# A new order of steps, new engine flags and new buffer numbers for a two-layer attention kernel on one Trainium2 core

## The chip, the cores and the metric

The kernel runs on one core of a Trainium2 chip. The metric is device time in microseconds (us), measured over whole executions. The engines are TensorE (PE, matrix products), VectorE (DVE), ScalarE (ACT), GpSimd (POOL) and SyncE (SP), which issues transfers (DMA). PEld in a profile is TensorE's weight load, which overlaps PE.

## What is computed

Two attention mixers alternate over x, which has 2048 rows of 512 bf16 values: A, B, A, B, each with layer normalisation ahead and a residual addition behind. Both layers A share their weights, and so do both layers B. There are 32 heads of 16 channels.

```python
def A(x):   # linear attention
    pq, pk = q @ w_phi, k @ w_phi
    phi_q = concat(softmax(pq), softmax(-pq))   # 32 features
    phi_k = concat(softmax(pk), softmax(-pk))
    kv = phi_k^T v                              # over all rows
    z = sum of phi_k over all rows
    return (phi_q kv / (phi_q z + 1e-6)) @ wo

def B(x):   # each row sees 8 rows: itself and 2, 4, ... 14 rows back
    attn = softmax(q . k[idx] / 4, masked where idx < 0)
    return (sum over the 8 of attn * v[idx]) @ wo

x = x + A(ln(x)); x = x + B(ln(x)); x = x + A(ln(x)); x = x + B(ln(x))
```

## The kernel before

x stays in on-chip memory as four blocks b of 512 rows, each with four tiles t of 128 rows. All of the kernel is built from small steps. A step belongs to one engine and issues a few instructions. Function names start with `s_`, and a step's name says its stage, layer L and block b.

- Head: `s_loads` queues the loads of x and the raw weights on SP (L315 to L327), `s_consts` sets constants and issues 14 matmuls that only warm PE (L287), `s_ln_first` normalises the first x, `s_fold` folds `w_phi` into the query part (fold0) and the key part (fold1) of the weight: transposes (L364), a product with `PHI` (L374) and a cast into `WA`.
- Layer A: `s_a1` makes keys (L593) and values (L605), exponentials (L599), their sums and reciprocals, the scaled keys (L651) and the sum kv over all rows (L668). `s_a2` makes the queries (L698), their exponentials `Eq` (L706) and sums (L714). `s_akv` turns kv over once all blocks are in: a cast, transposes (L744), and the products that form `ZM` (L753) and `R` (L757). `s_a3` makes the scale factors `rho` (L782 to L801). Blocks 0 and 1 spread `rho` over partitions by matmuls (L808) and multiply it into `Eq`: DVE either reads PSUM itself (L816), or ACT first copies it to `bs` (L846). Blocks 2 and 3 write `rho` to memory (L824), read it back as `Prho` (L831) and multiply by that (L835). `s_a4` takes the output product (L900) and `s_out`.
- `s_out`: a projection (L520) and the residual addition, either on DVE (L533) or by one more matmul with the identity (L523) and ACT (L530). Squares (L540) and sums give the next normalisation, applied by DVE (L444) or ACT (L446). xn is transposed by PE (L460) with a copy out of PSUM (L190 on DVE, L192 on ACT), or by a DMA transpose on SP (L451).
- Layer B: `s_b1` makes q, k and v (L927), cast out of PSUM by the shared helper `copy` (L190 or L192), and 4 DMAs for a group (L988) that spread V as `Vg`. `s_b2` multiplies q with the eight shifted k (`prod`, L1019), sums over channels on PE (L1026), takes exponentials (L1033), denominators (L1042) and the weights `PT` (L1054). `s_b3` multiplies by `Vg` (`pav`, L1081), sums on PE (L1090) and calls `s_out`. In the second layer B, results are stored (L544), and `s_flag` (L1115 to L1132) checks that no value went out of range.

Nothing is scheduled at run time. Each engine runs its instructions in the order in which the program issues them, and that is read from a table. A step that may run on DVE or on ACT (for residual additions: DVE, or PE and ACT) takes its flag from a second table, and each tile of the pools `big`, `med`, `t2` and `ps` (the eight PSUM banks) takes its buffer number from a third:

```python
def flex(self, stage, fn, *args):
    k = self.nflex
    self.nflex += 1
    self.step(stage, "F%d%s" % (k, fn.__name__), fn, *args, _CHOICE[k] == "1")
...
def slot(self, kind):
    k = self.ntile[kind]
    self.ntile[kind] = k + 1
    return kind + _SLOTS[kind][k]
...
for w in _ORDER.split():
    key = self.names[int(w, 36)]
    i = n.get(key, 0)
    n[key] = i + 1
    self.threads[key][i]()
```

Of the kernel before, what the change touches and what calls it, by code (L numbers as in the profile page):

```python
# [54 lines left out]


_ORDER = """
av 8 i i i i i i i i i i i i 0 f 0 g e 2t 0 bs 9 h a d c 0 j k t i i j l 27 o p 3 3 d6 b 1x 1x t 1y o m 2 2 1q
1z 1x 1x q u t r 1q v x w n s 1r w 1s 4 20 y 21 1x 22 1x 23 1q 1q 1q 1q 1v 1w z 3d 3d 3d 1u 1t 25 3e 3e 3e z 5
3e 3e z z 26 10 18 18 d5 1 z 16 11 4i 15 6 1h 13 3d 3e 3e 25 25 26 18 25 18 12 26 26 28 26 26 26 26 19 12 28  # L60
2a 28 1h 18 14 12 12 1a 28 1c 3e 2g 2g 1f 2h 2h 1h 1h 1b 1i 2b 1b 1e 1d 29 2j 2k 1h 1j 1n 2r 1b 1l 2s 1b 2c 2r
1k 2s 17 2g 2g 2h 2h 1k 1k 2h 2h 2h 2h 2d 1g 2d 2d 2d 2e 2j 1m 35 36 32 2o 2o 33 2s 33 32 33 33 2r 2s 2s 1o 2o
2o 2d 2r 3a 1k 3a 1p 2p 2o 24 24 2s 24 2u 2v 35 37 2u 2u 2u 2s 2i 2w 2j 3a 2s 3a 2l 2z 2j 24 32 32 34 2m 3b 33
3d 3f 3f 2z 2z 2z 33 2f 33 33 2f 2f 2f 3a 3a 2q 2q 2q 30 3a 2n 3a 3a 2z 3e 2q 2x 35 35 b6 3b 3a 2y 31 31 31 31
3c 3c 38 3c 39 3c 3m 3f 3n 3o 3o 3o 24 24 3g 3g 3g 3f 3p 3q 3g 3g 3g 3g 3g 3r 3q 3f 3g 24 3h 3i 3i 5l 5m 5n 3p
3s 3q 3j 3k 3k 3t 3q 3p 3x 5m 3w 3u 3h 3i 3i 3q 3v 3q 3q 3y 3h 3i 3q 3i 3h 3i 3q 5l 5o 5p 5r 5m 5q 7 7 3z 3q
3i 3j 3k 5m 5l 5s 3k 7 7 5m 5m 5m 3h 3i 7g 40 5u 44 41 42 5t 5m 5m 3j 3j 7h 7i 3k 5v 5m 5w 43 7h 45 7j 45 60
3k 3k 3k 46 45 45 5y 5x 5z 61 61 48 47 47 61 49 47 4a 47 4b 62 47 4b 63 3j 4g 94 4c 45 4d 45 4e 4f 3k 45 45 61
64 63 4h 4p 65 95 7j 7j 66 4q 63 96 95 97 97 63 67 7h 63 67 69 7h 6b 4k 4k 4k 4l 4p 4r 4k 4m 4p 4p 4s 4t 7k 7n
6a 68 6c 4o 7m 50 50 4u 4u 4u 4n 4u 7l 4w 97 7o 7p 7p 7q 7s 3l 4x 7r 7r 7p 7t 7p 6o 7u 50 7r 7r 7v 6o 6j 4v 4y  # L70
4j 6o 6q 6o 4j 4z 6k 6p 6r 6j 7r 6e 6l 95 6d 95 7v 6t 6s 6f 6d 7w 6e 7z 7x 98 9b 9a 99 6g 7y 9c 6e 6j 6j 9d 9d
6u 9d 6e 6n 80 6m 9d 6h 6v 6v 9e 9h 9f 6i 9g 9f 6w 6v 6v 6w 6w 9f 9i 9f 87 88 8h 9j 9f 50 82 9j 9l 6w 6x 6x 87
87 6w 81 83 9n 6x 9k 87 8b 89 51 51 51 51 52 52 8c 8c 8e 6u 6u 6u 9m 8j 8a 8d 8c 6v 6y 3l 8f 82 9o 82 85 82 50
51 52 4z 4z 4z 9q 9q 9s 8c 6z 8g 6y 6z 9r 71 70 6y 6y 6z 6z 72 86 a0 a0 a1 73 84 8i 74 75 74 74 50 74 8i 76 8i
77 a2 76 79 53 53 54 55 54 a5 56 53 54 9v 78 76 9q 9q 76 a0 81 53 9v 9w 9p 7a 57 9v 9u a7 76 7a 9t 8j 7c 9y 54
58 59 59 59 9v 59 9x 7d 7e 5a 8j 8j 7b 7f 5c 5b 5d 5b 5b a0 8k 5e 5b 5f 8k 9z a7 5b 5f 5j 8k 8k 8l a3 5i b4 a4
b7 5h b4 b4 b4 8l 5g b5 b5 a7 b5 b5 a7 8k 8l 8j c3 8i c3 b8 c4 c4 c4 c4 a8 8m a8 a8 a8 c3 a9 a9 5k at c1 b5 a6
8m au au c1 c2 b5 c2 aw c2 c2 a8 a9 b5 b5 8n 8o 8n 8p 8m at au at at 8n 8q 8m a7 aa 8n aw 8r 8s au au au 8s 8s
8t au au 8s 8v a6 a6 8u aa 8w aa 8x 8u 8u 8u 8y ab ac ab ad a6 aa b7 8u b9 b7 c3 8y 90 92 c1 91 c1 c2 8z c2 c2
aw ay ab c2 ba ae ab af aw b0 c4 c4 b1 bc ag ag ag ag ah bc aj ak bc c1 c4 c4 bc al ax c3 ai ai ai bd b1 ai am  # L80
93 bf bi bg az bf ai am ar bf bf bg bg aq b7 bg bg bg bg bg bb an ao ag ag ap bi ag ag b1 b1 bc b2 c2 bi bn bi
bl bk as bq br br bq br br bq bq b1 br by by by by bt b3 b3 b3 b3 br be be be br br bz c5 c5 bh bj bn bn bn c5
bu c4 by by by by c6 bo by c6 c6 c5 bt bt bt bn bv c6 c6 c6 bz be bp bp bw bm bp bp c0 c0 by c6 c6 bx c0 c0 c9
c5 ca c6 cb cb cc cb cd ce cd fr fs c7 c8 c7 c8 c8 ft cc ci cf cd cg cd c7 c8 c8 fs fu c8 e2 fu ch cd e3 cd cc
cj ck e4 cd c7 c8 c8 c7 e3 e2 cm cd c8 e6 e7 fu cl cd cd cn cp co e5 e3 hb e3 cr e2 ea e9 cq hc cs e3 cs e8 e3
e3 hd eb ec e3 e3 e3 ed ct cv hc eh cs he ee cs ef cw eg ei cx ei ei cu ei cu cu cu fs cy fs fv ej cu cy d0 cz
ek d2 fw fx fz d3 cs cs fy cs cs g0 g0 g0 el ek em ek en ek d4 d1 dc g1 eo ek g2 g3 g2 dc de eo es g0 g4 dd dh
g2 g5 g2 he hc eq g6 d7 d8 d7 d7 d7 he di dc g2 dc d9 ep er hc et dn hf da db df dh dh dh hi hh hj hg hk hk hk
dj dk dl dm dm g6 g7 g9 dn dn dg ga f0 f0 hl hm hn hm ho hm ev ew f1 hk dn g8 do do hp f2 fa fc hm hq do do dp
ev ex fc gb ev f0 dp ey dn f3 f0 hm fc f4 hq ev ez fc do dp dn dq dq d6 f5 f6 dm dm eu hs gi gj gi fd gs hr fd  # L90
ht fd hu hv fd dq fe fe f5 f5 f8 f5 f9 f7 fb gk fd fe fc gn gn gp gi gi gl gm gd gd gd ge ic gf i7 i7 i9 gg i8
dr dr dt ds dr du hx hy gd dq gu dr dv gn gq gh i7 ff ia gu fb go ff fg fh fb fb eu gv gc gn i2 gr i3 hx hz hx
i7 i2 ib gv i4 hx i1 gc hw i2 i2 i5 gu i0 gu gv gv gw gt ie fg fi if i6 ie id gw if dw dx id gv gw id id ie ie
if if ig dw ff ig if ig fg fj dw e0 dw ff fg fk ie fl fm fl fn gu fl fl fp ih ih ih ih e1 ii ii ii ik ij fq dy
gt gt gt fo fo il io io io io ii im ip iq ip is ir ir ih ii in ip ip iu it ir gx ir gy gx gx gx gz gy h0 dz dz
iv gy h1 h4 gx gy h2 h4 iw iv h5 h5 h6 h7 gy h4 h3 h5 h8 h9 h7 h7 h4 h5 ha h7
"""


_CHOICE = (  # L100
    "0011111111111001110111111010000010010000000000000001011111101100100000110101000110000010000001110111"
    "1101011110010000110101000000000000001101011000000000100100000000000000000101111100000011011000000000"
    "0000000000001101111010000000100101011111010000011001110111000000000000000111111011101110010100101000"
    "00000000000001111001000000000000000000000000000000000000000000000000000000000001111"
)


_SLOTS = {
    "big": (
        "0123456701231231456204632073205712053720457604356704213560421356720415763215063506432506"  # L110
    ),
    "med": (
        "0123456789abcdef5837ae98eeaeae471853bc9e43cbe47199ce3185413cebf94c8f74e3581bc71931bc7f370bf9ac21584e"
        "af9c37214a0b589dec37"
    ),
    "t2": (
        "0123450123450342150132451032451032451032451302153421530421503452014520345123045130425123504321504321"
        "5043215043210451023134"
    ),
    "ps": (  # L120
        "0123456701234750613250746132074365462150743510635127035164051362731405263710452763210743562107423251"
        "0764376215043762435107625407152367423167052341760543210675432170652147053624036542076314257603415203"
        "6415026734107534105234065265346053460562036207346201542015471204712603712035764120356471032516407324"
        "6735012463754021637261350247613025476130746513072463501742635017463015276301562703152760432764327014"
        "6570324650324705613245076"
    ),
}

# [1689 lines left out]
```

## Time and profile before

| | us |
|---|---|
| runs | 330.14, 329.95, 328.3 (median 329.95) |
| span of the profiled execution | 327.5 |
| TensorE busy | 310.3 (95%) |
| VectorE busy | 302.2 (92%) |
| ScalarE busy | 279.3 (85%) |
| GpSimd busy | 25.3 (8%) |

The profiled execution's own time beside its span isn't among the data; its span lies 0.8 to 2.6 us under the three runs. The granted clock of TensorE is at full speed in nearly all slices. A timeline row reads: start, duration, engine, source line, operation, output<-input, shapes, count, and in brackets the idle time before it with what ended it. A row of groups reads: line, engine, operation, shapes, count | busy us, mean ns of one | idle time before them.

### The profile page before, as it was taken

To read this page: it belongs to the slowest core of one execution; us is meant where nothing else is said; L and a number is where in the kernel's file an instruction comes from. 1 tells how busy PE (TensorE), PEld (TensorE's weight loads), DVE (VectorE), ACT (ScalarE), POOL (GpSimd) and SP (SyncE) were. 2 spreads that over 40 slices of the span, in tenths; PEclk is the share of its full clock that TensorE was granted. 3 is DMA by queue.
4 is the path that set the end of the run, shared out by engine and by line. 5 is a ranking of instruction groups with operands and counts; after the bars stand their busy time and mean duration, and the time that the engine had idled before them with its cause. 6 is when DMAs were issued, how large, how long until landed. Compare 5 with 4: busy or idle time off the path is not lost. (4 is left out here: it accounts for less than half of the span.)

```text
span 327.5 us, 8033 instructions
## 1 busy us (share of the span) xinstructions
PE 310.3 (95%) x3176; PEld 149.5 (46%) x3203; DVE 302.2 (92%) x439; ACT 279.3 (85%) x634; POOL 25.3 (8%) x50
## 2 busy tenths in 40 slices
PE   7999999999999999999999999979999999999873
PEld 3655456445444444443444455644544454433221
DVE  7998995998998999899999999699999999999993
ACT  5999988998888999989999999798999996676550
POOL 4000000000021003000000000000000208400000
PEclk9999999999999999999999999999999999999999
DMA  7980000004556899998750300023436977679952
GB/s 197 380 197 3 0 2 4 2 20 120 105 148 135 152 164 133 139 121 154 137 135 1 67 3 2 4 59 90 128 58 125 179 146 134 150 139 158 166 176 92
DMA packets 37388, 35.41 MB, mean 108 GB/s; under 512 B 23008, under 2 KB 32224, under 8 KB 37344
## 3 DMA queue, kind: packets, MB, share of 16 engines
q1 hardware_dynamic: 36816, 34.81, 53.6%
q8 instruction: 27, 0.44, 0.6%
q14 instruction: 17, 0.14, 0.2%
q10 hardware_dynamic: 528, 0.02, 0.1%
HBM read 10.50 MB, written 2.36 MB: 39 GB/s over the span
## 5 line engine op out<-in xcount | busy, mean ns | idle before, releaser
L927 PE MATMUL ps<-xnT,WB 128*128 128x512 bf16 x384 | 87.6, 380 | 0.5 <-DMA xnT<-xn 0.5
L1081 DVE TENSOR_TENSOR pav<-PT,Vg 128x4096 bf16<-128x4096 bf16 (+1 forms) x34 | 72.0, 2162 | 1.5 <-DMA Vg<-V 1.0
L1019 DVE TENSOR_TENSOR prod<-QT,K 128x4096 bf16<-128x4096 bf16 x32 | 72.5, 2291 | 0.3 <-ACT QT L192 0.2
L927 PEld LDWEIGHTS <-WB 128*128 128x128 bf16 x384 | 42.3, 114 | 43.3 <-issue 5.8
L520 PEld LDWEIGHTS <-oT 128*128 128x128 bf16 x256 | 23.8, 97 | 34.5 <-ACT oT L192 5.7
L192 ACT CAST oT<-ps 128x512 bf16<-128x512 f32 (+1 forms) x60 | 32.1, 587 | 8.4 <-PE ps L1090 7.1
L706 ACT ACTIVATE Eq<-ps 128x512 bf16<-128x512 f32 x64 | 34.0, 615 | 0.7 <-PE ps L698 0.6
L520 PE MATMUL ps<-WoB,oT 128*128 128x512 bf16 x122 | 32.1, 380 | 2.4 <-ACT oT L192 2.0
L599 ACT ACTIVATE Ek<-ps 128x512 bf16<-128x512 f32 x64 | 33.6, 622 | 0.4 <-PE ps L593 0.2
L698 PE MATMUL ps<-xnT,WA 128*128 128x512 bf16 x128 | 30.7, 380 | 0.6 <-DVE Eq L816 0.6
L540 ACT ACTIVATE sqd<-x 128x512 bf16<-128x512 bf16 x48 | 30.1, 643 | 1.0 <-DVE x L533 0.8
L605 PE MATMUL ps<-WA,xnT 128*128 128x512 bf16 x120 | 30.0, 380 | 0.5 <-issue 0.2
L593 PE MATMUL ps<-WA,xnT 128*128 128x512 bf16 x124 | 29.7, 380 | 0.6 <-DMA xnT<-xn 0.2
L520 PE MATMUL ps<-WoA,oT 128*128 128x512 bf16 x120 | 29.2, 380 | 0.4
L533 DVE SCALAR_TENSOR_TENSOR x<-ps,x 128x512 bf16<-128x512 f32 x38 | 25.4, 686 | 1.9 <-PE ps L520 1.7
L192 ACT CAST V<-ps 128x512 bf16<-128x512 f32 x31 | 17.5, 595 | 4.4 <-PE ps L927 4.3
L192 ACT CAST K<-ps 128x512 bf16<-128x512 f32 x31 | 17.8, 585 | 3.7 <-PE ps L927 3.3
L530 ACT ACTIVATE x<-ps 128x512 bf16<-128x512 f32 x26 | 15.1, 598 | 6.4 <-PE ps L523 6.3
L192 ACT CAST QT<-ps 128x512 bf16<-128x512 f32 x29 | 17.1, 592 | 2.5 <-PE ps L927 2.5
L651 DVE TENSOR_TENSOR Ek<-Ek,rk 128x4096 bf16<-128x4096 bf16 (+1 forms) x10 | 18.6, 1858 | 0.5 <-ACT rk L646 0.5
L593 PEld LDWEIGHTS <-xnT 128*128 128x128 bf16 x128 | 12.1, 97 | 15.4 <-DMA xnT<-xn 0.7
L446 ACT ACTIVATE xn<-x,nmr,rstd 128x512 bf16<-128x512 bf16 x23 | 18.2, 822 | 1.0 <-DVE nmr L435 0.8
(129 smaller groups left out, 433.3 us busy)
## 6 DMA issues: line engine op xcount, KB each, us to landing
Vg<-V SPq DMA_DIRECT2D x128, 131.5 KB, 4.4
Prho<-rd SPq DMA_DIRECT2D x8, 512.0 KB
x<-in_A_x_dram SPq DMA_DIRECT2D x3, 512.0 KB
WB<-in_B_wqkv_dram SPq DMA_DIRECT2D x3, 512.0 KB, 11.6
wraw<-in_A_wqkv_dram SPq DMA_DIRECT2D x4, 256.0 KB, 4.5
out_dram<-x SPq DMA_DIRECT2D x4, 256.0 KB, 2.2
out_dram<-x SPq DMA_DIRECT2D x8, 128.0 KB, 2.2
x<-in_A_x_dram SPq DMA_DIRECT2D x4, 128.0 KB
```

The costliest lines, as they stand in the source:

```text
L192: self.nc.scalar.copy(out=out, in_=in_)
L520: nc.tensor.matmul(y[:], lhsT=oT[:, c, t * P:(t + 1) * P], rhs=Wo()[:, c, :], start=(c == 0), stop=(c == NB - 1 and not onpe))
L533: nc.vector.scalar_tensor_tensor(out=xb[:, t, :], in0=T[t][:], scalar=1.0, in1=xb[:, t, :], op0=ALU.mult, op1=ALU.add, **kw)
L540: nc.scalar.activation(out=sqd[:], in_=xb[:, t, :], func=ACT.Square, accum_out=T["ss"][:, t:t + 1])
L593: nc.tensor.matmul(pk[:], lhsT=xnT[:, t, k, :], rhs=self.WA[:, k, D:2 * D], start=(k == 0), stop=(k == NB - 1))
L599: nc.scalar.activation(out=T["E"][:, t, s, :], in_=T["k", t][:], func=ACT.Exp, scale=1.0 - 2.0 * s)
L605: nc.tensor.matmul(pv[:], lhsT=xnT[:, t, k, :], rhs=self.WA[:, k, 2 * D:3 * D], start=(k == 0), stop=(k == NB - 1))
L698: nc.tensor.matmul(pq[:], lhsT=self.WA[:, k, hb * P:(hb + 1) * P], rhs=xnT[:, :, k, :], start=(k == 0), stop=(k == NB - 1))
L706: nc.scalar.activation(out=self.Eq[L, b][s][:, :, hb, :], in_=T[hb][:].rearrange("p (t i) -> p t i", t=4), func=ACT.Exp, scale=1.0 - 2.0 * s)
L927: nc.tensor.matmul(pp[:], lhsT=self.WB[:, k, i * D + c:(i + 1) * D:NB], rhs=xnT[:, :, k, :], start=(k == 0), stop=(k == NB - 1))
L1019: nc.vector.tensor_tensor(out=pr[:], in0=QT[:, c:c + 1, :].to_broadcast([P, NW, TB]), in1=win, op=ALU.mult)
L1081: nc.vector.tensor_tensor(out=pv, in0=PT[:, :, lo:lo + n].unsqueeze(1).to_broadcast([P, NB, 2, n]), in1=vw, op=ALU.mult)
```

## The change

Three tables are replaced, and nothing else: `_ORDER` (1452 steps, the same ones in another order), `_CHOICE` (383 flags, of which 118 are set in place of 124) and `_SLOTS` (the buffer numbers of 425 PSUM tiles, 122 `t2` tiles, 120 `med` tiles and 88 `big` tiles).

```diff
 _ORDER = """
-av 8 i i i i i i i i i i i i 0 f 0 g e 2t 0 bs 9 h a d c 0 j k t i i j l 27 o p 3 3 d6 b 1x 1x t 1y o m 2 2 1q
...
+9 8 2i i i i i i i i i i i a b i c i i i 3 1x 0 2t j k 0 0 0 o p j l 1y t t m o 3 1x q u 2 1q 1r 2 r n 1q 1z 1x
...
 _CHOICE = (
-    "0011111111111001110111111010000010010000000000000001011111101100100000110101000110000010000001110111"
...
+    "0111110111010111111101111010100010100001100000010010001110110100100000100111000000001000000011111000"
...
 _SLOTS = {
     "ps": (
-        "0123456701234750613250746132074365462150743510635127035164051362731405263710452763210743562107423251"
...
+        "0012345012345067405621473056473401563745630467054672307314250135010230145671326045710234607156201456"
...
```

Read as steps, the start of the order changes like this. Before: `c_zero`, the warming matmuls, loads of x tiles 0 to 3, then the raw query weight, the raw key weight, x blocks 1 and 2, the value weight and x block 3. After: the warming matmuls, the first half of the raw query weight, its transposes, x tiles 0 to 3, its second half, the raw key weight, x block 1, the value weight, x blocks 2 and 3. The first projection is of queries (L698) before and of keys (L593) after. Of the flags, products read from PSUM by DVE (L816) go from 25 to 21, normalisations applied by DVE (L444) from 41 to 38, copies of transposed blocks by DVE from 11 to 12; casts out of PSUM by DVE stay at 19 and residual additions by PE at 26.

More of the change, by code (lines that the diff above doesn't have):

```diff
@@ L57 @@
 _ORDER = """
-av 8 i i i i i i i i i i i i 0 f 0 g e 2t 0 bs 9 h a d c 0 j k t i i j l 27 o p 3 3 d6 b 1x 1x t 1y o m 2 2 1q
[L59 to L96, printed above, removed]
+9 8 2i i i i i i i i i i i a b i c i i i 3 1x 0 2t j k 0 0 0 o p j l 1y t t m o 3 1x q u 2 1q 1r 2 r n 1q 1z 1x
@@ new lines @@
+1x 1x 20 t bh s 1s 1x e 1q 1t 1q 1q v 1q 1v w x w 1w y 1u 25 26 25 25 25 22 4 z z z 26 z 21 10 z 15 13 1 11 28
+28 23 5 12 28 12 12 16 12 26 26 26 26 3d 3d 26 26 2a 3e 3e 18 18 18 18 14 2b 28 19 6 av 2g 2g 1h 2c 4j 1h 1h 1h
+17 2h 2h 3e 2h 2h 18 1a 3d 3d 1c 1i 1h 1j 1o 1e 2j 3e 3e 3e 2j 3e 3e 1b 1n 1b 1d 2g 1b 1f 2g 1b 2d 1g 1l 2h 2h
+2h 1k 2d 2d f 1k 1m 1k 1k d 2r 2h 2k 2u 2r 2r 2s 2d 2s 2e 2s 2s 2o 2o 2o 1p 2u 2w 2r 2s 2s 2s 2s 29 32 2o 2d 2z
+27 2p 2o 33 35 36 2v 35 37 35 33 32 33 33 32 3j 3k 3k 7 3a 2j 3f 2j 3a 3a 3a 33 2l 32 3b 2m 3f 33 33 2z 2z 2z 3a
@@ new lines @@
+33 3d 2u 2u 30 3a 3a 3a 3a 38 2z 2n 35 2f 3g 3g 2f 2f 3b 2f 2q 2q 2q 2q d5 31 2y 34 39 31 3e 2x 31 31 3c 3a 3c
+3c 3c 3m h 3f 3n g 3g 3g 3g 3g 3o 3f 3o 3o 3g 3g 3p 3q 3r 3h 3i 3f 3g 5l 3q 3p 3i 3v 3s 3q 3j 3u 3p 3k 5m 5n 3t
+3q 3q 3k 3q 7 3w 5m 3h 3y 3z 3i 3q 3h 3h 3x 3q 3q 3i 3i 5l 3q 3i 5r 5q 3j 5o 24 5m 5l 3i 24 24 3i 24 5p 5m 24 7
+3h 24 5m 5t 5m 5u 3i 40 42 41 44 5s 5m 5v 5m 5m 5m 7g 7h 43 3j 5w 5x 7i 7h 7 45 45 46 7j 7j 7j 5z 45 45 5y 48 60
+61 61 61 3k 3k 3k 47 49 4a 47 47 47 4b 47 4b 61 4c 4d 4g 45 45 4f 45 45 64 3k 3j 4h 94 4e 4k 4u 4k 3k 62 63 24
@@ new lines @@
+95 65 63 96 4l 66 4u 95 63 63 4m 97 97 7h 4v 4w 4p 4p 4p 67 4u 4q 7h d6 63 67 69 4r 68 6b 6a 7k 7m 7n 4k 4n 4s
+4k 4o 4p 7l 4u 4i 50 50 50 7o 7p 7q 3l 7p 7p 7s 7t 7p 4y 6c 6j 4x 4t 6j 6j 7r 7r 7r 7u 7r 6l 95 6e 97 6e 7v 7r
+7v 7y 6o 7w 7z 4z 4z 6k 6f 6e 6h 6p 6j 6g 6o 6o 6o 7x 80 6n 6q 95 6s 6r 6m 6e 98 9c 99 4j 6d 6u 9a 51 50 6t 6v
+6v 51 51 51 52 52 9b 6v 9d 9e 6i 6v 6u 50 6u 82 9f 83 9d 87 9d 9g 3l 9d 9h 9f 9i 6d 6w 6w 6w 6w 9f 88 8h 9f 9j
+9f 9j 9m 9l 8c 9n 6x 6x 87 6w 9k 82 82 6x 8d 87 87 8j 8a 8b 8c 89 6v 6y 6y 51 52 8c 8f 85 9o 50 9v 9v 9x 9q 9r
@@ new lines @@
+9q a5 9s a0 a1 9w 6y 8e 9q 6z 6z 6u 71 6z 6y 70 4z 4z 6z 72 73 b6 8c 8g 74 74 74 74 9v 53 82 9t 54 75 76 53 53
+53 77 84 78 76 76 79 76 7a 54 54 81 8i 55 8i 8j 76 7a 7b 54 7e 57 86 56 a0 a0 8i 8j 58 8j a2 7d 7c 59 9q 5a 5b
+59 59 59 5c 5b 5d a0 5b 8k a7 5e 5b 5f 8k 8k 8k 9y 5b 5f 5j 5h 5g 9v 9u 7f b4 8i b7 b7 9z 5i a7 a7 c3 8l 8l a4
+b7 a7 b8 b9 8k 8l 5k a3 c3 8j 8m 8m 8m 81 a8 a8 a8 c4 c4 a8 c4 c4 a9 at 9p ba a9 a6 a6 au au aw aw aw az ax a8
+a9 at au au at au at c1 ay au au au 8n 8o 8n 8n 8m a7 a6 8n 8q c2 c2 8p c1 8r aa aa aa aw c2 c2 b5 b5 b4 8s 8t
@@ new lines @@
+8s 8s 8s 8w b0 8v b4 a6 8u 8u 8u 8x aa c3 c3 ab ab ab b5 b5 8u 8y 8u ab ac 8y 91 92 90 b4 ad 8z 93 ae b1 af ag
+ah ag ag aj ak b5 b5 b5 ag b5 c4 ai ai ai al bc ai am bc bs bc bc c1 c2 c4 c4 ai am an b7 bf bg ar ao aq bg bi
+bj c4 bf bi bg bd ag ag ag ag bg b1 bi bl ap bq bq as bq br br br br br b1 b1 bb bc bq by by by bt b2 bf bk b1
+br bg bf bg by bg bg bn bt bt bt bz bw b3 b3 b3 c2 bx bn b3 be bv be be br bn bn be br by by bo c7 c8 c5 c5 c6
+c6 bu c6 bi c6 c1 bn bp bp by by by bz c2 c2 c5 c5 c6 c6 bm bp bp c0 c0 c6 c6 by c0 c0 c1 c9 ca cb cb cb c2 c5
@@ new lines @@
+cc c6 c3 cd ce fr cd cc c4 fs ci cf cd c8 cg cd ft fs ch cc cl cj cm e2 e3 e4 c7 c8 c8 cd cd c7 c8 e3 ck cd cd
+cd cd e2 e5 e3 e7 c8 c7 cn c8 c8 cq hb e6 e8 cr cp c7 c8 e3 co e2 e9 eb e3 cs cs ec ct cu e3 e3 ea e3 e3 e3 hc
+hd fu fu ed ef cv cs cs eg eh ee ei ei ei hc cu cw fu fs fs cu fv cx cu cy cu ei he fw ej cy fx fz d3 he cz d0
+cs cs fy em g0 g0 d2 cs g1 cs g0 g0 en ek el ek ek d1 d4 d7 dc g2 ek hc eo ek eo ep eq er d8 es dc dc g4 dc dg
+dd df de fa d7 d9 g3 g2 dh dh dh g5 di g2 he hc hf g2 hj d7 da dk hg dn dn d7 db g6 g2 dn et f0 f1 f0 f2 ev ew
@@ new lines @@
+ev dh g6 g9 g8 dn f0 hi dj dl d6 do do dm do do dm hh hk hk f3 fc ex fc ev dp dp dn g7 hl ga gb hm hk ey hn hm
+ho do dp hk hp fc dm dm dn hm hm hq f5 f6 f5 f5 ev dq f0 hm hq gd dq ez f4 fc ht f5 f9 f7 dr ds eu f8 eu fd fd
+fd hs hu gi gj hr gn gn go dr gp dq fd dq gd gd gi dt ge gi fe fe fd gk gs gu gf gu gg gd fe fb gl gn gq fc gh
+gi gm hv i2 i3 dr dr dv ic du fb fb gc i7 i7 i9 fb gv gv gn gr gt i2 gc i2 hx hy i5 i4 gu hx hx i7 gu hz i2 i7
+i6 i0 gt i8 ff fg ff fg fi ie ie hx if i1 gv gv ie ie ib hw ia id id if if gw ff gw id gv dw ff fh gw if ig ig
@@ L97 @@
+if id ig gu fg fj ie dw fg fk dx fl dw dw e1 fl fn fl fp gx gy gz ih ii ih ij ii ik fl fq ih ih gt gt fm fo fo
+ii il ii im io io ih e0 ii ip iq ir ip is ir gx gx gx gx io in dy dz dz iv gy h0 ip it io ip iu gy h1 gy h4 h4
+ir iw iv h2 ir h5 h6 h7 gy h3 h5 h8 h4 h5 h4 h5 h7 h9 h7 ha h7
 """
 _CHOICE = (
-    "0011111111111001110111111010000010010000000000000001011111101100100000110101000110000010000001110111"
-    "1101011110010000110101000000000000001101011000000000100100000000000000000101111100000011011000000000"
@@ L103 @@
-    "0000000000001101111010000000100101011111010000011001110111000000000000000111111011101110010100101000"
-    "00000000000001111001000000000000000000000000000000000000000000000000000000000001111"
+    "0111110111010111111101111010100010100001100000010010001110110100100000100111000000001000000011111000"
+    "1101100111000000110000000000000000001111100100000000000000001000000000001100111100100000011100000000"
+    "0000100000001111110000000100010000011110100100010011111010000000000010000111111011100100001001010000"
@@ L105 @@
+    "00000000000001111001000000001000000000000000000000000010010000000000000000000001101"
 )
 _SLOTS = {
-    "big": (
[L110 to L114, printed above, removed]
+    "med": (
+        "0123456789abcdef15466339715535a029d4bc6359dc4b0b26c4523907916bc274f25034f19b62fcbcf6665ce76028bf1903"
+        "468ce2fb1650793a82ce"
+    ),
@@ new lines @@
+    "ps": (
+        "0012345012345067405621473056473401563745630467054672307314250135010230145671326045710234607156201456"
+        "7102501260354235740123014567120456017612345601234506203201342013412512012412410561045672301207123723"
+        "4567153427104571274012375410230450236123163123456340350723403643501502520120145672031401356724501732"
+        "5047602317062134570132140256701230456176301306723012012301450165075072312013012301345367364562674012"
+        "3121040450402041020320412"
+    ),
@@ L115 @@
+    "big": (
+        "0123456701234561234506273456027315024731560247165027341650273041627530461046531204512670"
     ),
     "t2": (
[L117 to L120, printed above, removed]
-        "0123456701234750613250746132074365462150743510635127035164051362731405263710452763210743562107423251"
[L122 to L125, printed above, removed]
+        "0123450000011112223444444444444444555550120350000000001321452444444442222244444031115555200000000000"
+        "0004443144452150302415"
```

## The prediction

> **What bounds the kernel now.** I read the page first, for the three engines that carry the work, then the table by stage, then the timeline at the joints between stages.
>
> ```profile
> span 327.5 us, 8033 instructions
> PE 310.3 (95%) x3176; PEld 149.5 (46%) x3203; DVE 302.2 (92%) x439; ACT 279.3 (85%) x634; POOL 25.3 (8%) x50
> ...
> PE   7999999999999999999999999979999999999873
> ...
> DVE  7998995998998999899999999699999999999993
> ```
>
> TensorE (PE) is busy for 310.3 of 327.5 us and VectorE (DVE) for 302.2, so at most 17.2 us of idle PE time can be won by any order at all. The slices put the gaps at the start, in slice 27 (213 to 221 us) and at the end.
>
> ```profile
> 40.00:60.00 20.00, 19.45 (x473) 11.26 (x473) 15.68 (x28) 17.33 (x40) 0.38 (x1) 1.00 0.01 2
> ...
> 160.00:180.00 20.00, 19.90 (x136) 8.11 (x137) 19.68 (x21) 19.21 (x47) 0.00 (x0) 1.00 0.45 84
> 200.00:220.00 20.00, 18.25 (x465) 10.58 (x465) 16.55 (x32) 17.54 (x41) 0.00 (x0) 1.00 0.08 20
> ...
> 280.00:300.00 20.00, 18.75 (x148) 7.98 (x148) 20.00 (x10) 14.23 (x31) 3.61 (x2) 1.00 0.87 152
> ...
> 320.00:328.00 8.00, 2.16 (x16) 0.69 (x8) 2.56 (x4) 0.37 (x1) 0.00 (x0) 0.90 0.23 75
> ```
>
> The columns are the stretch, its length, then busy time (and instructions) of PE, weight loads, DVE, ScalarE (ACT) and GpSimd, the granted clock, the DMA share and GB/s. Four kinds of stretch follow. From 40 to 60 us PE sets the pace: DVE is idle for 4.3 of 20 us. In the middle (160 to 180) PE, DVE and ACT are all within 0.8 us of full. At 200 to 220, where layer A's second attention is turned over (I call it switch 1; switch 0 is the same place in the first layer, near 53 us), PE lies idle for 1.75 us and DVE for 3.45: a chain of small steps sets the pace. From 280 to 300 DVE is full and PE has 1.25 us to spare. The clock is 1.00 in all of these but the last, so no throttle is at work.
>
> **The change part by part.** No instruction is added or removed; the list of steps, the engine flags and the buffer numbers differ. TensorE gets exactly the same matmuls (the number of residual additions made on PE is 26 in both). These are the groups that change size:
>
> ```profile
> L446 ACT ACTIVATE xn<-x,nmr,rstd 128x512 bf16<-128x512 bf16 x23 | 18.2, 822 | 1.0 <-DVE nmr L435 0.8
> ...
> L816 DVE TENSOR_TENSOR Eq<-ps,Eq 128x512 bf16<-128x512 f32 x25 | 16.1, 682 | 0.1
> ...
> L444 DVE TENSOR_SCALAR xn<-x,rstd,nmr 128x512 bf16<-128x512 bf16 x41 | 14.9, 408 | 0.4
> ...
> L190 DVE COPY xnT<-ps 128x1024 bf16<-128x1024 bf16 (+1 forms) x11 | 7.2, 661 | 0.7 <-PE ps L460 0.6
> ...
> L846 ACT CAST bs<-ps 128x512 bf16<-128x512 f32 x7 | 4.1, 589 | 0.0
> ...
> L190 DVE CAST oT<-ps 128x512 bf16<-128x512 f32 x6 | 4.0, 685 | 0.3 <-PE ps L900 0.3
> ...
> L192 ACT COPY xnT<-ps 128x1024 bf16<-128x1024 bf16 (+1 forms) x4 | 3.8, 945 | 0.2 <-PE ps L460 0.2
> ...
> L816 DVE TENSOR_TENSOR Eq<-bs,Eq 128x512 bf16<-128x512 bf16 x7 | 2.9, 416 | 0.0
> ```
>
> *Engine choices.* Products read straight from PSUM go from 25 to 21, so four go through an ACT copy first: DVE 4 x (0.682 - 0.416) = -1.06 us, ACT 4 x 0.589 = +2.36. Applications of the normalisation go from 41 to 38 on DVE: -3 x 0.408 = -1.22, ACT +3 x 0.822 = +2.47. One copy of a transposed block goes from ACT to DVE: +0.66, -0.95. PSUM casts on DVE stay at 19. Sum: DVE -1.6, ACT +3.9, PE 0. ACT has 48 us of idle time, so its load alone costs nothing; where it is late next is the second rival. What DVE saves counts only where DVE sets the pace, so I go by place, counting the changed steps there.
>
> *Head.* Before, the first projection is the query one, which needs only one third of the folded weight.
>
> ```profile
> 0.81 1.82 SPq L315 DMA_DIRECT2D x<-in_A_x_dram  x4
> 1.27 5.30 PE L287 MATMUL ps<-kvT 128*128 128x512 bf16 x14 [1.27 <-DVE kvT L242]
> 9.79 3.85 ACT L192 CAST WA<-ps 128x512 bf16<-128x512 f32 x7
> 11.61 2.75 PE L698 MATMUL ps<-xnT,WA 128*128 128x512 bf16 x12
> ```
>
> The new order sends the query weight's first half ahead of x, transposes it first, and begins with a key projection (L593), which needs the key part of the fold: four casts of 3.85 / 7 = 0.55 us. In the old run the last of the seven ended at 13.64 us, and one issue more (1.82 / 4 = 0.45) now stands ahead of x on SyncE's queue. From below: the 0.45 us are lost inside the 5.30 us of warming matmuls and the casts are ordered earlier, -0.6; from above: 0.45 and two casts late, +1.5. I take +0.5, near the row of the one issue that surely moves.
>
> *Switches.* From the product that forms ZM to the first `prod`:
>
> ```profile
> 53.70 0.29 DVE L753 TENSOR_TENSOR ZM<-ps,maskH 128x32 bf16<-128x32 bf16 x2 [0.57 <-PE ps L744]
> 85.16 2.28 DVE L1019 TENSOR_TENSOR prod<-QT,K 128x4096 bf16<-128x4096 bf16 x1
> ...
> 209.28 0.29 DVE L753 TENSOR_TENSOR ZM<-ps,maskH 128x32 bf16<-128x32 bf16 x2 [1.87 <-PE ps L744]
> 241.17 2.29 DVE L1019 TENSOR_TENSOR prod<-QT,K 128x4096 bf16<-128x4096 bf16 x1
> ```
>
> Each takes 31 to 32 us. In switch 0 two products move to the ACT path, and one application and one cast leave DVE: -0.53 - 0.41 - 0.69 = -1.6. Against it, one more query group of four matmuls stands ahead of the transposes that ZM waits for: by the 2.75 us for 12 this is 4 x 0.23 = +0.9. PE is the fuller engine there, so the saving can be worth nothing; between -0.7 and +0.9 I take 0. In switch 1 again two products move and one cast leaves, and one residual addition of 0.69 joins: -0.5.
>
> What the switches may pay is the round trip by which blocks 2 and 3 get their scale factors: rho is written to memory and read back as Prho (512 KB each, two for a block) before the products of L835. The worst case is block 3 of the second layer:
>
> ```profile
> 223.60 0.41 DVE L801 TENSOR_TENSOR rho<-rS,Ds 128x256 bf16<-128x256 f32 x1
> 229.00:237.30 8.30, 8.08 (x79) 4.13 (x78) 7.58 (x23) 7.78 (x22) 0.00 (x0) 1.00 0.42 126
> 237.64 1.22 DVE L835 TENSOR_TENSOR Eq<-Eq,Prho 128x2048 bf16<-128x2048 bf16 x1
> 240.04 1.22 DVE L835 TENSOR_TENSOR Eq<-Eq,Prho 128x2048 bf16<-128x2048 bf16 x1
> ```
>
> 126 GB/s for 8.30 us are the two transfers. The first half of these bytes is through at 233.2, 9.1 us after rho ends at 224.0; all of them at 237.3, 13.3 us after. The products waited for neither, at 13.6 and 16.0 us. DVE's own work between rho and the two products counted step by step at the groups' durations, falls from 11.9 to 8.4 us and from 14.1 to 12.2 us in the new list. With the 1.8 us that DVE idled there, that is 10.2 and 14.0: just behind the bytes. Bounds: 0 if the bytes decide, and 13.6 - 8.4 = 5.2 if they land only when the old products began. I take +0.4, since the bytes are measured. Switch 1 is then -0.1.
>
> *Middle,* from the first `prod` to the second ZM: three applications and one cast fewer on DVE, 3 x 0.41 + 0.69 = -1.9, and the same matmuls on PE. With PE at 19.90 of 20 us the matmuls cover it: 0. If that cover were gone, up to -1.9; if the reordering adds waits to PE, +1, about twice the 0.55 us that PE lost in the row of 40 to 60 us.
>
> *Last run and tail.*
>
> ```profile
> 317.71 1.22 DVE L1081 TENSOR_TENSOR pav<-PT,Vg 128x2048 bf16<-128x2048 bf16 x1
> 320.10 2.08 PE L520 MATMUL ps<-WoB,oT 128*128 128x512 bf16 x8
> 322.22 0.69 DVE L533 SCALAR_TENSOR_TENSOR x<-ps,x 128x512 bf16<-128x512 f32 x1 [0.35 <-PE ps L520]
> ```
>
> Here DVE is full, so one application less, -0.4, counts whole. After the last `pav` PE has nine output matmuls in place of eight (+0.2) and DVE five residual additions in place of four, the last of which already waits for PE. Bounds 0 to +0.9; I take +0.2.
>
> **Sum:** +0.5 + 0 - 0.1 + 0 - 0.4 + 0.2 = +0.2 us on a span of 327.5. One thing is left that I cannot place: PSUM. In the old list a bank is written again at most two projection groups after its last write (8 x 0.216 = 1.73 us of matmuls) 44 times, in the new one 110 times. Where ACT is late, PE now stands. Only the second rival prices it in full; a tenth of an ACT cast for each of the 27 more that lie in the switches and the middle, where PE is full, is 27 x 0.06 = 1.6; between 0 and that I add 0.3. The span is then 328.0. The profiled execution lies 2.45 us under the median of the runs (329.95), so the median becomes 330.4.
>
> Now a rule that speaks against the new head. By the rows above, 12 full matmuls took 2.75 us (0.23 each) right after 5 us of transposes and small matmuls, while the 14 warming ones took 5.30 us (0.38 each). The Trainium skill, TensorE: Matmul & The Clock Gate, Part 1, says that the clock halves after an idle window of about 3.4 us, and its Part 4 that transposes don't count as busy in the same way. By that rule the first 3.4 us of projections would again run at 0.38; the row of 2.75 us shows that they did not.
>
> **The rivals.** *Faster: DVE sets more than I think.* If DVE's savings count in full wherever they lie, -1.6 - 0.5 - 1.9 - 0.4 = -4.4, and with +0.7 for head and tail the change is -3.7: 326.2. For it: DVE is at 19.68 of 20 in the middle and full at the end, and PE's 1.75 us at switch 1 are waits for DVE's chain. Against it: PE at 19.90 of 20. It decides if PE's idle time in the middle and the switches halves.
>
> *Slower: banks come back too early.* 27 more early reuses where PE is full; a drain by ACT takes 0.59 us behind the last matmul's 0.38, so one instruction ahead of it on ACT fits into 1.73 us, and a second (0.59 more) does not. ACT is busy for 19.21 of 20 us in the middle and gets 3.9 us more work. If half of the 27 pay half a cast, 13.5 x 0.29 = 3.9 us: 334.3. Against it: the order puts each drain where ACT comes free. It decides from the point where two ACT instructions stand ahead of a drain. Late Prho transfers would show in the same place with up to 5.2 us.
>
> *No effect from the order, but a cold head.* If the first projections ran at 0.38 in place of 0.23 us for 3.4 us, 9 matmuls lose 0.15 each, 1.4 us: 331.8. The rows above speak against it. The Trainium skill's page TensorE: Matmul & The Clock Gate, Parts 1 and 4, would give this case.
>
> **How the numbers follow.** Forecast 0.48, cold head 0.03, faster 0.20, banks or Prho late 0.29. A measurement of this kernel can tell about 1% (3.3 us) from no change; the forecast and the cold head fall within it, the faster rival (-3.7) and the slower one (+4.4) outside. Chances: faster 0.20, same 0.51, slower 0.29. The forecast's own range is 328.1 to 332.6: the distances to the bounds (head 1.1 and 1.0, switch 0 0.7 and 0.9, middle 1.9 and 1.0, banks 0.3 and 1.3, tail 0.2 and 0.7) added as squares, since nothing ties them. The whole range reaches to the faster rival with the head's lower bound, 326.2 - 0.6, rounded to 325.5, and past the slower one by half of its price, 336.0.
>
> **What would show it.** Right: PE's busy time stays within 1 us of 310.3 and DVE's falls by about 1.6 while ACT's grows by about 3.9; the first L593 starts near 12.1 us; ZM to first `prod` takes 30 to 32 us in both switches; the products L835 of block 3 start 10 to 14 us after rho with at most 1 us of waiting for Prho; PE's waits for ACT stay under 5 us in total. Wrong: PE idle time behind ACT drains grows by more than 3 us (slower), DVE waits named Prho of over 2 us, or PE idle under 13 us in all (faster).

## The result, and the profile after

The changed kernel takes 334.56 us (median of four runs, 332.28 to 336.0) against 330.04: a ratio of 1.0139, 95% interval 1.0091 to 1.0188. Run once more beside the experiments, it had 1.0169 (1.0156 to 1.0182), 5.6 us. It is slower by 1.4%, between 0.9 and 1.9%. The forecast of 330.4 was 4 us short: the time lies above the forecast's own range (328.1 to 332.6) and inside the whole one (325.5 to 336.0).

The page of the changed kernel, its lines on span, busy time and clock:

```profile
span 332.4 us, 8071 instructions
...
PE 313.8 (94%) x3203; PEld 150.6 (45%) x3203; DVE 300.1 (90%) x436; ACT 284.7 (86%) x641; POOL 30.5 (9%) x50
...
PE   7999999999999999999999999798999989998793
...
DVE  5999995897979899998999999499899999999993
...
PEclk9999999999999999999999999979999999999998
```

DVE's work fell by 2.1 us and ACT's rose by 5.4; the span grew by 4.9. PE's 3.5 us more are in part records that the first trace lacks (3176 of 3203) and in part the dip of the clock in slice 27 (216 to 224 us): a second profile of the changed kernel, with 3178 records and no dip, has 310.4. So DVE's work went down as it was meant to, and the time between pieces of work went up.

Cut at the same events in both kernels (first projection, first ZM, first `prod`, second ZM, first `prod` of the second layer, end of the last `pav`), the table by stage reads, first for the kernel before:

```profile
0.00:11.60 11.60, 9.89 (x94) 6.38 (x95) 9.79 (x35) 7.47 (x15) 4.35 (x28) 1.00 0.83 250
11.60:53.70 42.10, 41.73 (x498) 22.32 (x500) 37.94 (x71) 39.60 (x85) 0.77 (x2) 1.00 0.29 83
53.70:85.15 31.45, 30.79 (x482) 15.69 (x498) 27.64 (x67) 28.46 (x69) 0.00 (x0) 1.00 0.17 43
85.15:209.28 124.13, 122.08 (x1131) 57.20 (x1116) 117.64 (x136) 115.98 (x269) 7.27 (x11) 1.00 0.62 104
209.28:241.17 31.89, 29.51 (x430) 15.11 (x434) 29.20 (x70) 28.75 (x76) 0.00 (x0) 1.00 0.26 72
241.17:318.92 77.75, 73.03 (x545) 31.75 (x549) 76.93 (x57) 58.54 (x124) 12.91 (x9) 1.00 0.81 149
```

and for the changed kernel:

```profile
0.00:12.40 12.40, 9.89 (x94) 6.29 (x95) 8.63 (x31) 6.70 (x13) 4.01 (x26) 1.00 0.85 255
12.40:55.50 43.10, 42.80 (x506) 22.95 (x504) 39.71 (x77) 39.91 (x85) 0.46 (x2) 1.00 0.27 72
55.50:86.31 30.81, 30.23 (x480) 15.36 (x494) 26.15 (x65) 29.75 (x71) 0.31 (x2) 1.00 0.18 47
86.31:211.88 125.57, 123.44 (x1091) 57.53 (x1083) 116.29 (x133) 118.44 (x271) 9.92 (x11) 1.00 0.65 103
211.88:245.04 33.16, 30.41 (x492) 15.54 (x489) 28.77 (x69) 29.43 (x73) 0.00 (x0) 0.95 0.28 71
245.04:323.43 78.39, 73.69 (x550) 31.68 (x549) 76.75 (x53) 60.10 (x132) 15.79 (x9) 1.00 0.82 147
```

The second number is the length. The differences are +0.8, +1.0, -0.6, +1.4, +1.3 and +0.6 us, and 0.4 behind the last `pav`: no single place holds the loss, and only switch 0 got shorter. Some of it is work that crossed a cut: a query group of four matmuls (0.9 us) now stands ahead of each ZM, so most of the +1.0 and of the -0.6 is the same group. In the middle DVE does 1.35 us less in 1.4 us more. What it waited for is in its list of waits (total, times, longest), first before, then after:

```profile
DVE ZM L753 <- PE ps L744: 2.4, 2, 1.9
...
DVE q L552 <- ACT sqd L540: 1.1, 2, 0.8
...
DVE nmr L435 <- ACT rstd L431: 0.3, 1, 0.3
```

```profile
DVE ZM L753 <- PE ps L744: 4.9, 2, 2.6
DVE q L552 <- ACT sqd L540: 4.2, 8, 1.1
DVE nmr L435 <- ACT rstd L431: 3.4, 6, 0.7
...
DVE Eq L835 <- DMA Prho<-rd: 1.1, 1, 1.1
```

In the normalisation DVE waits for ACT's squares and reciprocal roots: 7.6 us in 14 waits, 1.4 us in 3 before. Eight of the 14 waits, 3.5 us, lie in the middle, where the kernel before has none. Squares and roots are ACT's in both kernels, so DVE doesn't wait for the moved steps themselves; that ACT is late because it has more to do is a reading of the traces.

The last line is one wait of the middle, for block 3 of the first layer, whose second product with Prho found its data late:

```profile
99.17 1.23 DVE L835 TENSOR_TENSOR Eq<-Eq,Prho 128x2048 bf16<-128x2048 bf16 x1 [1.12 <-DMA Prho<-rd]
```

In the kernel before, both products run without a wait:

```profile
96.03 2.39 DVE L835 TENSOR_TENSOR Eq<-Eq,Prho 128x2048 bf16<-128x2048 bf16 x2
```

In the second profile of the changed kernel this wait is 1.97 us, 0.85 longer. There the middle takes 126.43 us, 0.86 longer, and the waits of DVE behind this row start 0.95 to 0.97 us later than in the first profile, where the steps ahead of it start 0.10 later. So a wait of DVE at this place goes through to the end of the middle, although PE is nearly full by its records. All seven profiles of kernels with the new middle show this wait (0.89 to 1.97 us), and none of the five with the old middle, the two swaps of flags left out. Why the data came late isn't settled: the read back was issued 8.9 us after rho ended, 9.4 before, but the transfers of `Vg` followed it after 2.7 us in place of 5.1.

### The profile page after: what moved, and what is told of

Read it like the earlier page. It is cut to its first block, busy times and chain, and to the rows that moved or that the text cites. A ratio compares the mean times of both kernels' runs of the same rounds, so it can differ in the third digit from the quotient of the medians.

```text
span 332.4 us, 8071 instructions
## 1 busy us (share of the span) xinstructions
PE 313.8 (94%) x3203; PEld 150.6 (45%) x3203; DVE 300.1 (90%) x436; ACT 284.7 (86%) x641; POOL 30.5 (9%) x50
## 4 chain that ended last, share of the span: by engine, by line
PE 40%; ACT 21%; DVE 18%; DMA 10%; issue 5%; SPq 4%; ACTq 0%; DVEq 0%
PE ps L520 8%; PE ps L927 7%; DVE prod L1019 6%; PE ps L605 6%; PE ps L593 5%; DMA Vg<-V 5%; PE ps L698 4%; ACT sqd L540 4%; ACT Eq L706 3%; SPq L988 3%; DMA Prho<-rd 2%; ACT oT L192 2%; DMA xnT<-xn 2%; DVE Ek L651 2%; ACT Ek L599 2%
## 5 line engine op out<-in xcount | busy, mean ns | idle before, releaser
L192 ACT CAST oT<-ps 128x512 bf16<-128x512 f32 (+1 forms) x58 | 31.2, 587 | 6.0 <-PE ps L1090 4.9
L706 ACT ACTIVATE Eq<-ps 128x512 bf16<-128x512 f32 x64 | 34.7, 615 | 0.6 <-PE ps L698 0.6
L599 ACT ACTIVATE Ek<-ps 128x512 bf16<-128x512 f32 x64 | 34.5, 622 | 0.0
L698 PE MATMUL ps<-xnT,WA 128*128 128x512 bf16 x128 | 32.9, 393 | 0.0
L605 PE MATMUL ps<-WA,xnT 128*128 128x512 bf16 x128 | 31.2, 379 | 0.1
L593 PE MATMUL ps<-WA,xnT 128*128 128x512 bf16 x128 | 30.8, 379 | 0.1
L520 PE MATMUL ps<-WoA,oT 128*128 128x512 bf16 x128 | 30.5, 379 | 0.3 <-ACT QT L192 0.2
L446 ACT ACTIVATE xn<-x,nmr,rstd 128x512 bf16<-128x512 bf16 x26 | 20.6, 824 | 1.6 <-DVE nmr L435 1.6
L192 ACT CAST QT<-ps 128x512 bf16<-128x512 f32 x32 | 18.7, 592 | 2.9 <-PE ps L927 2.9
L1090 PE MATMUL ps<-pav,indAV 128*32 128x512 bf16 (+1 forms) x272 | 17.9, 370 | 2.8 <-DVE pav L1081 2.8
```

Of the source, the lines that this page charges most:

```text
L192: self.nc.scalar.copy(out=out, in_=in_)
L520: nc.tensor.matmul(y[:], lhsT=oT[:, c, t * P:(t + 1) * P], rhs=Wo()[:, c, :], start=(c == 0), stop=(c == NB - 1 and not onpe))
L593: nc.tensor.matmul(pk[:], lhsT=xnT[:, t, k, :], rhs=self.WA[:, k, D:2 * D], start=(k == 0), stop=(k == NB - 1))
L599: nc.scalar.activation(out=T["E"][:, t, s, :], in_=T["k", t][:], func=ACT.Exp, scale=1.0 - 2.0 * s)
L605: nc.tensor.matmul(pv[:], lhsT=xnT[:, t, k, :], rhs=self.WA[:, k, 2 * D:3 * D], start=(k == 0), stop=(k == NB - 1))
L698: nc.tensor.matmul(pq[:], lhsT=self.WA[:, k, hb * P:(hb + 1) * P], rhs=xnT[:, :, k, :], start=(k == 0), stop=(k == NB - 1))
```

## The experiments

**Banks.** `_SLOTS` of the changed kernel, its `ps` line only:

```diff
-    "ps": "0012345012345067405621473056473401563745630467054672307314250135..."
+    "ps": "0123456701423756275631204756172064175201570265016253176051473520..."
```

> The new order and flags, with the PSUM bank numbers given out anew so that each tile takes the bank that has been free longest. If banks that come back too early cost the time (the second rival of the prediction), this wins 2 us or more back: 332.5 or less, and PE's waits at bank reuse go. If the loss lies in the order itself (head, two switches, a halved clock), it stays within 0.7 us of the changed kernel, 334 to 335, some 4.5 us over the kernel before.

Measured: 338.57 us, 1.0264 (1.0235 to 1.0292). It is not faster than the changed kernel but 3 us slower, though banks come back later: in the `ps` table, 36 tiles take a bank that one of the four tiles ahead of them had, 119 in the changed kernel and 17 before. The rival that came nearest to the measured time, 334.3, falls as it was stated. The trace suggests why at one place, near 110 us in the middle. In the changed kernel PE waits there for banks:

```profile
111.42 1.02 PE L927 MATMUL ps<-xnT,WB 128*128 128x512 bf16 x4 [0.47 <-DVE x L533]
112.65 1.89 PE L520 MATMUL ps<-WoA,oT 128*128 128x512 bf16 x8 [0.21 <-ACT QT L192]
...
118.06 0.90 PE L1042 MATMUL ps<-E,indDen 128*128 128x512 bf16 x2
```

(its second profile, of the run `again` below), and with the banks spread these waits are gone and another stands behind them:

```profile
111.23 1.03 PE L927 MATMUL ps<-xnT,WB 128*128 128x512 bf16 x4
112.09 1.89 PE L520 MATMUL ps<-WoA,oT 128*128 128x512 bf16 x8
...
118.45 0.38 PE L1042 MATMUL ps<-E,indDen 128*128 128x512 bf16 x1 [0.78 <-ACT E L1033]
```

PE gets to L1042 no sooner: ACT's exponential sets that time. Here the waits at banks hid a wait for ACT. What made the rest of the 3 us isn't settled.

**The halved clock.** In the profile of the changed kernel, switch 1 runs small matmuls for 8 us, and then eight large ones, seven of them at 551 to 631 ns where others take 380:

```profile
216.87 3.33 PE L698 MATMUL ps<-xnT,WA 128*128 128x512 bf16 x8
...
218.00:220.00 2.00, 2.00 (x6) 0.44 (x4) 2.00 (x5) 1.58 (x4) 0.00 (x0) 0.50 0.16 33
```

The experiment moves one step of `_ORDER` up by 20 places, and gives 31 buffer numbers anew for it:

```diff
   a3_12.PE md
+  a2_13.PE mq(1)
   a3_10.DVE rho
   a3_10.PE bc(0)
...
   a3_11.ACT ln
-  a2_13.PE mq(1)
```

> The changed kernel with one query group of four matmuls of 512 columns (block 3, group 1) moved ahead of the first spreading of rho in switch 1, in among the small matmuls; the rest as it is. If the halved clock there follows from some 8 us without a large matmul, the clock stays at 1.00 and the 1.5 us that seven matmuls lost at 631 in place of 380 ns come back: 333.0. If the clock falls for another reason, the rows of 631 ns stay and so does the time, 334.5. If the chain of small DVE and ACT steps sets switch 1, the clock stays up but the time doesn't fall.

Measured: 336.19 us, 1.0205 (1.0172 to 1.0237), with no matmul slower than 408 ns behind the 14 warming ones. The clock stays up and the time doesn't fall: the third of the expectations. The second profile of the unchanged table (below) settles it: there the same eight matmuls take 1.89 us at full clock, and the run is no faster. The halved clock was seen in one of two profiles. The eight matmuls took 1.44 us longer with it, but switch 1 as a whole only 0.45 (33.16 and 32.71 us), and the execution with the halved clock was the shorter one (334.24 and 335.59 us). The Trainium skill, TensorE: Matmul & The Clock Gate, Part 1, says that the window in which the clock is decided runs freely and isn't tied to the kernel; the two profiles, one with seven slow matmuls and one with none, fit this and don't show the window itself.

Where filler's time went is in its rows: the group fills the wait, and the second spreading then waits for DVE and the products of the next block for ACT.

```profile
213.96 1.04 PE L698 MATMUL ps<-xnT,WA 128*128 128x512 bf16 x4
...
216.28 0.40 PE L808 MATMUL ps<-rho,indB 32*128 32x128 bf16 x14 [0.72 <-DVE Eq L816]
217.33 0.63 PE L782 MATMUL ps<-Eq,ZM 128*32 128x128 bf16 x32 [0.66 <-ACT bs L846]
...
220.35 0.40 PE L808 MATMUL ps<-rho,indB 32*128 32x128 bf16 x16 [1.42 <-DVE rho L801]
```

**Flags alone, order alone.** The edits put one kernel's `_CHOICE` beside the other's `_ORDER`. Some 16 buffer numbers of `t2` follow in each, and the second, new order with old flags, still differs from the old flags in ten. The first edit:

```diff
 _ORDER = <old>
-_CHOICE = "0011111111111001..."
+_CHOICE = "0111110111010111..."
```

> The old order with the new engine flags alone. VectorE's waits for ScalarE in the normalisation grew from 1.4 us to 7.6 us in the changed kernel (q behind sqd, nmr behind rstd). If ScalarE's 3.9 us of extra work make these waits, they come with the flags: 332 or more. If the order makes them, the time stays within 1 us of the kernel before, 329 to 331.

> The new order with the old engine flags, but for those of the products out of PSUM, which the new order's bank use needs. If the flags cost the time, at least 2 of the 4.8 us come back: 332.5 or less. If the order does, it stays at 334 to 335.5.

Measured: 368.33 us (1.1174, 1.1156 to 1.1192) and 368.6 us (1.1194, 1.1174 to 1.1214). Both lie more than 33 us beyond any number that I had given. A flag that moves a step to another engine puts it into that engine's queue at the place in the list where it happens to stand; what it needs may not be there yet, and all behind it waits. With the new flags in the old order DVE waits:

```profile
DVE x L533 <- PE ps L520: 14.2, 13, 5.0
DVE Eq L816 <- ACT bs L846: 6.8, 3, 2.9
DVE q L552 <- ACT sqd L540: 6.1, 7, 2.3
```

So the question whether flags or order cost the 5 us has no answer from swapping them: the two tables belong together. That ACT's extra work makes DVE's new waits is read from the traces, and not shown by a run of its own.

**Pieces.** The two lists of steps hold nearly the same steps up to the switches (at the start of switch 1 they differ by 6 of some 980, at switch 0 by some 18 of 350), so a kernel can follow one list to there and the other from there, with flags and buffer numbers to match. Each joint is a place where steps that one list had already done and the other not are done together. The numbers of `t2` were given out anew, in part also where a piece keeps the old order.

```diff
 late_new:     old [0 .. switch 1]            + new [switch 1 .. end]
 early_new:    new [0 .. switch 1]            + old [switch 1 .. end]
 first_new:    new [0 .. switch 0]            + old
 middle_new:   old [.. first prod] + new [.. switch 1] + old
 switch1_new:  old [.. switch 1] + new [.. rho of block 3 written] + old
 last_new:     old [.. rho of block 3 written] + new
 switch1_old:  new [.. switch 1] + old [.. rho of block 3 written] + new
 again:        new
```

> The old order, flags and buffer numbers up to the transposes that begin switch 1, the new ones from there on. By PE's delays in the two traces, 3.1 of the 4.8 us arise after that place (2.4 in switch 1, 0.7 behind it): 333.0. If instead the changed kernel enters switch 1 in a bad state (its loss was prepared in the middle), this loses 1 us at most: 331.0 or less.

> The new order, flags and buffer numbers up to the transposes that begin switch 1, the old ones from there on: the complement. By PE's delays +1.7 us over the kernel before (head 0.8, switch 0 0.4, middle 0.5): 331.7, and the clock stays at 1.00 in switch 1. If the two halves only lose together, it equals the kernel before, 330.0.

> The changed kernel as it is, beside the same runs of the kernel before as the pieces below. Both theories: 334 to 335, so that the pieces can be added up against it on one chip.

> The old kernel with the new order, flags and buffer numbers only in switch 1, from the transposes ahead of ZM to the write of block 3's rho (some 19 us). In the changed kernel and in the run that is new from here on, PE stands 1.4 to 1.7 us before the first spreading of rho, where the old order has eight projection matmuls. If this place costs what PE's delays show, the time is 1.8 us over the kernel before, 331.6; if the full VectorE of the last run swallows it, 330.5 or less.

> The old kernel with the new order, flags and buffer numbers from the start to the transposes of the first switch (some 53 us); single GpSimd steps that only open a buffer for the second layer stay where the old order has them. PE's first projection came 0.8 us later in the changed kernel, and nothing until the switch gave it back. If a late start goes through to the end, +0.8: 330.3. If the old switch 0 has slack for it, 329.5.

> The old kernel with the new order, flags and buffer numbers only from the first prod to the transposes of switch 1 (some 87 to 209 us). The prediction has 0 here, since PE is nearly full. PE's delays grow by 1.6 to 2.4 us more than before in this stretch in the changed kernel: +1.8, 331.3.

> The old kernel with the new order, flags and buffer numbers only from the end of switch 1 to the end. The prediction has -0.4 + 0.2 here: 329.3. From the first prod of the second layer to the last pav the changed kernel took 0.6 to 1.2 us longer than the old one, with PE waiting 0.9 us and more for one DMA transpose: +1.0, 330.5.

> The changed kernel with the old order, flags and buffer numbers in switch 1 only, the complement of switch1_new. If switch 1 costs 2.4 us wherever it stands, 2.4 come back: 332.8. If the later run is full on VectorE and takes the gain away, 334.5.

| kernel | median us | ratio to before | 95% interval | us over before |
|---|---|---|---|---|
| again | 335.19 | 1.0169 | 1.0156 to 1.0182 | 5.6 |
| early_new | 333.78 | 1.0123 | 1.0099 to 1.0147 | 4.1 |
| late_new | 333.27 | 1.0102 | 1.0075 to 1.0129 | 3.4 |
| first_new | 332.03 | 1.0065 | 1.0051 to 1.0079 | 2.1 |
| middle_new | 332.21 | 1.0074 | 1.0059 to 1.0088 | 2.4 |
| switch1_new | 331.82 | 1.0067 | 1.0053 to 1.0081 | 2.2 |
| last_new | 332.37 | 1.0082 | 1.0064 to 1.0100 | 2.7 |
| switch1_old | 335.45 | 1.0204 | 1.0169 to 1.0238 | 6.7 |

Each ratio is to the kernel before on the same chip, three chips in all; the last column is the ratio's excess times 330. late_new, switch1_new and again came within 0.3 us of what was expected, early_new lost more than twice what I gave it, and first_new, middle_new and last_new lost 0.6 to 1.7 us more. switch1_old gave nothing back. The four pieces sum to 9.4 us, more than the whole. That suggests that a joint costs something itself.

If all joints cost the same, switch 1 put in (its cost e, two joints s: e + 2s = 2.2) and taken out (6.7 - 5.6 = -e + 2s) give s = 0.8 and e = 0.55. Then the pieces without their joints are 1.3 (first), 0.8 (middle), 0.55 (switch 1) and 1.9 (last), and the remaining stretch, switch 0, is 5.6 - 4.55 = 1.05. Two runs not used for this agree: late_new would be 0.55 + 1.9 + 0.8 = 3.25 (measured 3.4), early_new 1.3 + 1.05 + 0.8 + 0.8 = 3.95 (4.1).

This is an estimate, and a loose one. The joints differ in size, and two of switch1_old's six runs, at 337.6 and 338.9 us, make its 6.7; by medians it is 5.75, and s falls to about 0.6. The two halves alone (4.1 + 3.4 - 5.6 = 2s) give 0.95. Over these values of s the first stretch costs 1.2 to 1.5 us, the middle 0.5 to 1.2, switch 1 0.3 to 1.0 and the last run 1.8 to 2.1, and what is left for switch 0, which has no run of its own, goes from -0.2 to 1.9. So the loss lies in several stretches; how it is shared out isn't shown.

Two waits within the pieces have names. Before the first spreading of rho the old order has eight projection matmuls:

```profile
210.54 1.90 PE L698 MATMUL ps<-xnT,WA 128*128 128x512 bf16 x8
212.37 0.40 PE L808 MATMUL ps<-rho,indB 32*128 32x128 bf16 x16
```

In switch1_new PE stands there, and later behind block 2's products, the second of which waits for Prho:

```profile
213.17 0.73 PE L808 MATMUL ps<-rho,indB 32*128 32x128 bf16 x32 [1.56 <-DVE rho L801]
...
227.80 1.04 PE L520 MATMUL ps<-WoA,oT 128*128 128x512 bf16 x3 [1.35 <-DVE Eq L835]
```

```profile
228.67 1.23 DVE L835 TENSOR_TENSOR Eq<-Eq,Prho 128x2048 bf16<-128x2048 bf16 x1 [0.89 <-DMA Prho<-rd]
```

In last_new PE waits for two DMA transposes:

```profile
PE ps L927 <- DMA xnT<-xn: 1.9, 2, 1.3
```

The shorter wait, 0.6 us, lies in the middle, as in the kernel before (0.5). The longer one, 1.3 us, is new and lies in the last run, where PE's waits for `pav` also grow, from 1.1 us in one wait to 3.1 in five.

In the changed kernel the transpose of the last run is issued at 260.37, behind a normalisation on DVE (259.47) that stands behind the `prod`s.

## Why the prediction was right or wrong

- **Head:** +0.5, measured +0.8 in the trace; the first L593 at 12.40 us in place of 12.1. Right, within its bounds. In five profiles with the old head the first projection starts at 11.61 to 12.47 us (median 11.76), in seven with the new head at 12.40 to 12.98 (12.56), again +0.8.
- **Switch 0:** 0, between -0.7 and +0.9. The group ahead of ZM shows in the stretch before it (+1.0), the lighter DVE and the missing group behind it (-0.6): +0.4. Right by the table; no run has this stretch alone.
- **Middle: the failed step.** I let PE cover all ("With PE at 19.90 of 20 us the matmuls cover it") and took 0 with bounds -1.9 and +1. Measured +1.4, and +2.3 in the second profile. PE is indeed busy for 123.44 of 125.57 us by its records, but it doesn't cover DVE's waits: the 0.85 us by which the wait for Prho differs between the two profiles come through whole. I priced three applications moved from DVE to ACT as work saved on DVE, and no wait that DVE would meet in the new order. It met 3.5 us for ACT in the normalisation and 1.1 (1.97) us for Prho. Which of these make up the +1.4 us, no run shows.
- **Late Prho:** I took +0.4 in switch 1, called block 3 of the second layer the worst case, and checked no other place. There nothing waited for Prho: the two products start 9.9 and 15.2 us after rho ends, the second with DVE at other steps until then. The waits came for block 3 of the first layer and, in the second profile, 0.92 us for block 2 of the second: 1.1 us in all in one profile and 2.9 in the other, past the 2 us that I had named as a sign of being wrong.
- **Switch 1:** -0.1, measured +1.3 (+0.8 in the second profile). DVE's work fell (28.77 for 29.20 us), but the moved projections left the chain from ZM to rho uncovered. I noted the order of PE's groups only for the one ahead of ZM and not for the two that left the wait behind it. ZM to the first `prod` takes 33.16 and 32.71 us, outside the 30 to 32 that I gave.
- **Last run:** -0.4, measured +0.6. DVE's busy time fell by only 0.2 us (76.93 to 76.75) and its idle time rose from 0.8 to 1.6: "Here DVE is full, so one application less, -0.4, counts whole" missed that DVE can be made to wait as well. The forecast's own range counts no bounds for this run, nor those of late Prho in switch 1.
- **Tail:** +0.2; with all behind the last `pav` +0.4.
- **Banks:** 0.3 taken, 3.9 as a rival. The sum of the rival was near the result and its mechanism was rejected by the run made for it. The trace had spoken against it already: PE's waits for ACT sum to 3.4 us before and to 3.2 and 3.8 in the two profiles after, where the rival needed over 3 us more. That the measured time fell inside the whole range is therefore luck: its upper part had been drawn for this rival. I had given 0.29 to slower.
- **Cold head:** the first projections ran at full clock after the transposes, as the rows of before had it. The 0.38 us that I took for a cold matmul is a mean: in the kernel before ten of the 14 warming matmuls are slow and four are not. The clock did halve once, elsewhere, in a stretch whose length differed by 0.45 us between the two profiles.

## What to carry to other kernels

In a program of in-order queues that is within 5% of its fullest engine, a sum of busy times tells what a new order could win, and says nothing of what it loses; for that, list for every moved step who waits for its result and where the same wait stood before. A full engine does not cover the waits of another: look at each place for the wait that ends last, and check a slow transfer wherever it is used, not only where it seems worst. Order, engine flags and buffer numbers belong together: the new flags in the old order cost 39 us, and a joint between two good orders some 0.6 to 1, by estimate.

## What the runs showed of the hardware that I had not expected

The same instructions met the halved clock in one profile (seven matmuls of 551 to 631 ns in place of 380, after 8 us of small matmuls) and not in the other, with no difference in time beyond the spread of the runs. Of the same 14 warming matmuls at the start, 7 to 13 took over 450 ns in the twelve profiles without the swaps of flags. And the head varies: in the profile of middle_new, which issues the same loads in the same order as the kernel before, the warming matmuls took 5.68 us in place of 5.30, TensorE's weight loads waited for the raw weights three times, 1.2 us in all, in place of once, 0.6 us, and the first projection came at 12.47 us in place of 11.61.
